# v for the pooled keys of the first two batches on all 128 partitions, both halves of v begun together, and an order planned with longer transfers

## The chip, the cores and the metric

The kernel runs on one core of a Trainium2 chip. The metric is the device time of one execution in microseconds. Three executions of the kernel before took 993.01, 996.15 and 1002.56 us; the median is 996.15 us. One further execution was profiled; it took 994.15 us, of which 991.8 us lie between its first and its last instruction (the span). All durations below come from that one execution.

## The reference, cut to what matters

There are 8 batches of 8 heads, 576 rows each of 64 numbers. Each head gets two attentions, and their outputs are added. The first averages q, k and v over groups of four rows (576 become 144), attends over all 144 pooled keys, and repeats each output row four times. The second attends only over keys at most three rows away. The sum, 4608 tokens of 512 numbers, goes through a two-layer network.

```python
q_d = q.reshape(B, H, Sd, factor, D).mean(axis=3)      # k_d and v_d alike; factor 4, Sd 144
out_d = sm_attn(q_d, k_d, v_d)
out_up = np.repeat(out_d, factor, axis=2)
scores = scale * np.matmul(q, k.transpose(0, 1, 3, 2))
scores = np.where(np.abs(pos[:, None] - pos[None, :]) < factor, scores, -1000000000.0)
out_local = np.matmul(softmax(scores), v)
x = (out_up + out_local).transpose(0, 2, 1, 3).reshape(4608, 512)
h = x @ w_in                                           # 512 x 2048
out = (h * np.clip(h + 3.0, 0.0, 6.0) / 6.0) @ w_out   # 2048 x 512
```

## The kernel before, in words

**Attention.** The work is cut into 32 units: batch b (0 to 7) and head pair hp (0 to 3). A unit keeps its two heads on the two halves of the partitions. `scores_d` (L401, L415 for later batches) multiplies pooled q with pooled k, `scores` (L569) multiplies windows of 64 rows for the local attention. Softmax follows: greatest value (L439) and sums (L448) on DVE (VectorE), exponentials on ACT (ScalarE; L435 pooled, L445 local), the tiny constant added on POOL (GpSimd, L451), the reciprocal on DVE (L454), the product with it on POOL or DVE (L457). Then the weights of the softmax are transposed, the pooled ones by L464 and the local ones by L592 on PE (TensorE) in batches 0 and 1 (`b < ALONE`). Later batches send them through DRAM (L476, L503 out; L484, L489, L510 back) and turn them on DVE (L498, L517). Last come the products with v (L543 pooled, L609 local), a scaling by a quarter on ACT (L548), and the addition of both outputs (`add`, L626) into x.

**v.** Each unit loads v twice. `ldv` loads the local windows: half h = 0 goes to partitions 0 to 63 as 64 x 5 x 128, half h = 1 to partitions 64 to 127 as 64 x 4 x 128 and 64 x 128. `ld4` loads the rows from which `sum4` (L369 on DVE, L371 and L372 on POOL) sums four and four. For batches 0 and 1 the 144 pooled keys stand as 72 and 72, even and odd keys, so these rows go to partitions 0 to 71 (`KB` is 72), and `trans_d` takes every second column.

**The network.** Tokens go in parts of 512, 256 and then 384 (`PART`). Each part has 16 first products (L864, one for each block of w_in, called wi0 to wi15) and 16 second products (L914, wo0 to wo15). All numbers are split into a high and a low fp32r part, so each product is three matmuls. `plan_split` makes the parts of x (high L119, low L791), L870, L874, L878 and L882 those of the hidden numbers.

**The weights.** A weight arrives as two 32-bit words (L161, 512 KB for a block of 128 x 512). ACT scales one word (L172 into a bank of PSUM, or L176 in place) and the other (L190), DVE puts the bits together (L181, L185), ACT rounds the high part (L195), POOL or DVE subtracts (L199). So each block costs ACT three instructions, and DVE two or three.

**What sets the order.** Every step is given to `Plan` with an engine, a cost in us, and what it waits for. `Plan.emit` runs a list schedule with these costs and writes each engine's instructions in the order that comes out. [...] `dma(packets, size)` is the cost of a transfer, `need(b)` the time at which a batch is wanted, `lag` an extra delay behind what a step waits for. While the plan sees PE idle at the start it fills the gap with matmuls that nobody reads (L947). `loads` lists the transfers of batch 0 for which the first `GATE` weight blocks wait; later blocks wait for the block `GATE` places ahead to be rounded. All transfers are issued by one engine, SP, in order. The tiles `early` are buffers of batch 0 that lie where weights go later; a0 to a2, o0 to o2, h0 and h1 are banks of PSUM.

## Time and profile before

| what | us |
|---|---|
| median of three runs | 996.15 |
| profiled execution | 994.15 |
| its span | 991.8 |
| PE busy in the span | 942.9 |
| DVE busy | 612.7 |
| ACT busy | 346.8 |
| POOL busy | 270.4 |

The page gives busy time by engine, 40 slices of the span with the busy share in tenths, the granted TensorE clock (PEclk) and what the transfers moved (GB/s), and the costliest groups. In an answer by time (a timeline), a row reads: start, duration, engine, line, operation, result and operands, and in square brackets how long the engine had idled before it and what ended that. In an answer on waits, a row reads: who waited for whom, us in total, how often, the longest. A table of stretches gives for each its length, then busy time of PE, PE's weight loads, DVE, ACT and POOL with the number of instructions, the granted clock (1.00 is full), the busy share of the transfer engines and GB/s.

### The profile page before, as it was taken

To read this page: it belongs to the slowest core of one execution; us is meant where nothing else is said; L and a number is where in the kernel's file an instruction comes from. 1 tells how busy PE (TensorE), PEld (TensorE's weight loads), DVE (VectorE), ACT (ScalarE), POOL (GpSimd) and SP (SyncE) were. 2 spreads that over 40 slices of the span, in tenths; PEclk is the share of its full clock that TensorE was granted. 3 is DMA by queue.
4 is the path that set the end of the run, shared out by engine and by line. 5 is a ranking of instruction groups with operands and counts; after the bars stand their busy time and mean duration, and the time that the engine had idled before them with its cause. 6 is when DMAs were issued, how large, how long until landed. Compare 5 with 4: busy or idle time off the path is not lost.

```text
span 991.8 us, 19738 instructions
## 1 busy us (share of the span) xinstructions
PE 942.9 (95%) x7493; PEld 811.4 (82%) x7493; DVE 612.7 (62%) x1147; ACT 346.8 (35%) x814; POOL 270.4 (27%) x370
## 2 busy tenths in 40 slices
PE   7689998997899999999999999999999999999997
PEld 4467776886788888888898888888898888998996
DVE  6688898677757576766736765766736753323322
ACT  4677664332322322322422322422322332322321
POOL 4644335123423223322402332432402320000000
PEclk9789999998999999999999999999999999999999
DMA  8977352456644545463524455453533430100101
GB/s 188 249 210 216 93 134 45 99 117 115 132 96 95 109 95 116 97 115 65 126 45 82 99 112 104 94 114 77 115 68 64 101 76 8 33 1 0 33 1 32
DMA packets 310974, 93.52 MB, mean 94 GB/s; under 512 B 251264, under 2 KB 297216, under 8 KB 310880
## 3 DMA queue, kind: packets, MB, share of 16 engines
q1 hardware_dynamic: 310880, 92.27, 42.6%
q8 instruction: 59, 0.97, 0.4%
q14 instruction: 35, 0.29, 0.1%
HBM read 69.60 MB, written 22.61 MB: 93 GB/s over the span
## 4 chain that ended last, share of the span: by engine, by line
PE 64%; SPq 11%; DMA 9%; DVE 9%; issue 3%; POOL 2%; ACT 2%; DVEq 0%; ACTq 0%; POOLq 0%
PE h L864 31%; PE o L914 28%; SPq L300 4%; DMA arena<-in_v_dram 3%; SPq L510 2%; SPq L484 1%; DMA arena<-pl 1%; DMA rawo<-in_w_out_dram 1%; SPq L489 1%; PE a L609 1%; DMA rawi<-in_w_in_dram 1%; PE a L569 1%; DVE arena L439 1%; DMA arena<-in_q_dram 1%; ACT arena L435 1%
## 5 line engine op out<-in xcount | busy, mean ns | idle before, releaser
L864 PE MATMUL h<-rounded,wi 128*128 128x384 f32 (+2 forms) x2240 | 438.4, 339 | 8.6 <-POOL rounded L791 3.7
L914 PE MATMUL o<-wo,rounded 128*128 128x512 f32 x1680 | 430.2, 396 | 4.9 <-ACT wo L195 1.2
L864 PEld LDWEIGHTS h<-rounded,wi 128*128 128x128 f32 x2240 | 391.6, 189 | 35.4 <-POOL rounded L791 4.0
L914 PEld LDWEIGHTS o<-wo,rounded 128*128 128x128 f32 x1680 | 308.1, 188 | 66.8 <-issue 4.2
L874 DVE SCALAR_TENSOR_TENSOR arena<-arena,h 128x384 f32<-128x384 f32 (+2 forms) x192 | 104.5, 546 | 154.5 <-ACT arena L870 153.8
L870 ACT ACTIVATE arena<-h 128x384 f32<-128x384 f32 (+2 forms) x192 | 94.0, 491 | 281.9 <-PE h L864 266.3
L878 ACT CAST rounded<-arena 128x384 fp32r<-128x384 f32 (+2 forms) x192 | 98.2, 513 | 173.7 <-DVE arena L874 116.6
L882 DVE TENSOR_TENSOR rounded<-arena,rounded 128x384 fp32r<-128x384 f32 (+2 forms) x154 | 90.0, 589 | 91.1 <-PE o L914 63.5
L882 POOL TENSOR_TENSOR rounded<-arena,rounded 128x384 fp32r<-128x384 f32 (+2 forms) x38 | 41.5, 1093 | 212.0 <-PE o L914 123.3
L435 ACT ACTIVATE arena<-a,arena 128x144 f32<-128x144 f32 x84 | 31.0, 377 | 101.2 <-DVE arena L430 82.0
L307 DVE STREAM_TRANSPOSE arena<-arena 128x576 f32<-128x576 f32 x56 | 42.7, 767 | 19.8 <-DMA arena<-in_q_dram 16.4
L442 POOL TENSOR_TENSOR arena<-arena 128x640 f32<-128x640 f32 x21 | 26.5, 1261 | 60.4 <-issue 36.3
L517 DVE STREAM_TRANSPOSE arena<-arena 128x640 f32<-128x640 f32 x24 | 20.2, 843 | 33.8 <-DMA arena<-pl 33.8
L609 PEld LDWEIGHTS a<-arena 64*64 64x64 f32 x1120 | 20.7, 134 | 20.9 <-ACT arena L435 8.6
L320 POOL TENSOR_TENSOR arena<-arena 128x144 f32<-128x144 f32 x23 | 12.0, 521 | 89.4 <-PE a L415 32.5
L451 POOL TENSOR_SCALAR arena<-arena 128x10 f32<-128x10 f32 (+1 forms) x60 | 16.7, 279 | 71.2 <-ACT arena L435 42.8
L609 PE MATMUL a<-arena 64*64 64x57 f32 (+1 forms) x1120 | 25.4, 223 | 11.1 <-ACT arena L435 7.6
L498 DVE STREAM_TRANSPOSE arena<-arena 128x384 f32<-128x384 f32 (+1 forms) x48 | 22.1, 466 | 17.1 <-DMA arena<-pd 16.5
L791 POOL TENSOR_TENSOR rounded<-arena,rounded 128x768 fp32r<-128x768 f32 x6 | 10.9, 1835 | 79.1 <-DVE rounded L121 79.1
L457 DVE TENSOR_TENSOR arena<-arena 128x432 f32<-128x432 f32 (+1 forms) x36 | 31.2, 868 | 0.9
L569 PE MATMUL a<-arena 64*64 64x64 f32 x1200 | 29.7, 226 | 0.5 <-ACT arena L119 0.5
L322 POOL TENSOR_TENSOR arena<-arena 128x144 f32<-128x144 f32 x46 | 28.7, 624 | 3.6
(182 smaller groups left out, 877.8 us busy)
## 6 DMA issues: line engine op xcount, KB each, us to landing
rawi<-in_w_in_dram SPq DMA_DIRECT2D x16, 512.0 KB
rawo<-in_w_out_dram SPq DMA_DIRECT2D x16, 512.0 KB
arena<-in_q_dram SPq DMA_DIRECT2D x112, 72.0 KB
arena<-in_k_dram SPq DMA_DIRECT2D x112, 72.0 KB
pl<-arena SPq DMA_DIRECT2D x24, 320.0 KB
arena<-pl SPq DMA_DIRECT2D x96, 80.0 KB
out_dram<-arena SPq DMA_DIRECT2D x96, 72.0 KB
arena<-in_v_dram SPq DMA_DIRECT2D x24, 256.0 KB
```

The lines of the kernel that those rows point to most:

```text
L300: nc.sync.dma_start(raw[32 * e:32 * e + 32], bass.AP(tensor=t.tensor, offset=t.offset + row0 * ROW + 32 * e, ap=[[ROW, 32], [32 * ROW, S / ...
L307: nc.vector.transpose(out=qk[kind], in_=st["raw", kind].rearrange("p j i -> p (j i)"))
L435: nc.scalar.activation(p[:, j], x[:, j], AF.Exp, bias=m[:, j:j + 1], scale=1.0 / 128.0, accum_out=s[:, j:j + 1])
L457: eng.tensor_tensor(x, x, s.unsqueeze(2).broadcast_to(list(x.shape)), op=ALU.mult)
L569: nc.tensor.matmul(st["ps", g][half:half + WIN, jj * D:jj * D + WIN], qk_of("q")[hs, k_first:k_first + WIN], qk_of("k")[hs, k_first:k_firs ...
L609: nc.tensor.matmul(st["px"][g][h * D:(h + 1) * D, at + lo:at + hi], st["v"][ks, jj, h * D:(h + 1) * D], st["pt"][ks, jj, half + lo:half + ...
L864: nc.tensor.matmul(st["ps"], win[f][:, wt, kk * P:(kk + 1) * P], xs[part][:, kk], start=(kk == 0 and i == 0), stop=(kk == NK - 1 and i == ...
L870: nc.scalar.activation(st["t"], st["ps"], AF.Relu, bias=3.0)
L874: nc.vector.scalar_tensor_tensor(out=t, in0=t, scalar=6.0, in1=st["ps"], op0=ALU.min, op1=ALU.mult)
L878: nc.scalar.copy(st["gh"], st["t"])
L882: eng.tensor_tensor(st["gl"], st["t"], st["gh"].bitcast(F32), op=ALU.subtract)
L914: nc.tensor.matmul(otile[n, m], gt[:, ms], wout[f][:, wt], start=(f == 0 and i == 0), stop=(f == NF - 1 and i == 2),)
```

## The change

The 144 pooled keys of batches 0 and 1 now stand as 128 and 16 in their own order, no longer as 72 and 72. So `ld4` loads the rows to be summed as one transfer to 128 partitions and one to 16, `sum4` makes sums of 128 and 16 partitions, `trans_d` takes columns 0 to 127 and 128 to 143, and `pv_d` multiplies over 128 and then 16. The number of instructions stays what it was on PE, DVE, ACT and POOL; batch 0 has one more transfer for each unit.

For batch 0 the second half of v no longer waits for the first, and both halves join `loads`. So the first ten weight blocks (`GATE` was 8) wait until all of batch 0 is loaded.

The plan's numbers change: `dma` costs 30% more, the pooled exponentials cost 1.74 in place of 1.0 (1.16 and 0.58 in place of 0.67 and 0.33 for later batches), ACT's first two steps on a weight come 2 us later (`LAGW`), and batch 1 is wanted 8 us sooner. The whole program is ordered anew by them.

```diff
-        a = op("ACT", 0.68, rebias, [ld], take=[place])
-        c = op("ACT", 0.68, low, [ld])
+        a = op("ACT", 0.68, rebias, [ld], take=[place], lag=LAGW)
+        c = op("ACT", 0.68, low, [ld], lag=LAGW)
...
         def ld4(g):
-            if b == 0:
-                raw = buf("raw4", ("v", un), [KB, 2, 4, ROW])
-                nc.sync.dma_start(raw, src(v_all, row0, [[8 * ROW, KB], [1, 8 * ROW]]))
-                st["raw", 0], st["raw", 1] = raw[:, 0], raw[:, 1]
-            elif alone:
-                st["raw", g] = raw = buf("raw" + k0, ("v", un, g), [KB, 4, ROW])
-                nc.sync.dma_start(raw, src(v_all, row0 + 4 * g, [[8 * ROW, KB], [1, 4 * ROW]]))
-            elif g == 0:
-                st["raw", g] = raw = buf("raw" + k0, ("v", un, g), [P, 4, ROW])
+            if b == 0 and "raw4" not in st:
+                st["raw4"] = buf("raw4", ("v", un), [P, 2, 4, ROW])
+            raw = st["raw4"][:, g] if b == 0 else buf("raw" + k0, ("v", un, g), [P, 4, ROW])
+            if g == 0:
                 nc.sync.dma_start(raw, src(v_all, row0, [[4 * ROW, P], [1, 4 * ROW]]))
             else:
-                st["raw", g] = raw = buf("raw" + k0, ("v", un, g), [NAR, 4, ROW])
-                for h in range(2):
+                n = 1 if alone else 2
+                raw = raw[:n * KR]
+                for h in range(n):
                     nc.sync.dma_start(
                         raw[h * KR:(h + 1) * KR], src(v_all, row0 + 4 * P, [[4 * ROW, KR], [1, 4 * ROW]]))
+            st["raw", g] = raw
...
-            lv.append(op("SP", 0.5, partial(ldv, h), lv[-1:], take=[("v" + kv, un)], size=dma(WIN * 5, 512), nd=1 + h))
+            lv.append(op("SP", 0.5, partial(ldv, h), [] if b == 0 else lv[-1:], take=[("v" + kv, un)], size=dma(WIN * 5, 512), nd=1 + h))
+        if b == 0:
+            loads.extend(lv)
...
-                nc.tensor.transpose(out=ps[:KB, j * P:(j + 1) * P], in_=st["pd"][:, j, g::2], identity=ident)
+                nc.tensor.transpose(
+                    out=ps[:nk[g], j * P:(j + 1) * P], in_=st["pd"][:, j, g * P:g * P + nk[g]], identity=ident)
...
-            sums_d = [op("ACT", 1.0, lambda: weigh(rows_d(), st["pd"], st["md"], st["sd"]), [a], free=[bk])]
+            sums_d = [op("ACT", 1.74, lambda: weigh(rows_d(), st["pd"], st["md"], st["sd"]), [a], free=[bk])]
...
-PRE, GATE = 4, 8
+PRE, GATE = 4, 10
...
+LAGW = 2.0
...
-    return start_of(need_chunk(b)) - (EARLY * TC if b and b % 2 == 0 else 0.0) - ((4.0, 16.0)[b] if b < ALONE else SLACK)
+    return start_of(need_chunk(b)) - (EARLY * TC if b and b % 2 == 0 else 0.0) - ((4.0, 24.0)[b] if b < ALONE else SLACK)
...
-    return packets * (5.0 + 0.0376 * size) / 16e3 if size > 256 else packets * (1.0 + 0.1 * size) / 16e3
+    return packets * (6.5 + 0.049 * size) / 16e3 if size > 256 else packets * (1.3 + 0.13 * size) / 16e3
```

What the new order does is shown at three places. Lines of the changed kernel are one or two off from those before (L443 is L445 before, L433 is L435, L455 is L457, L792 is L791, L865 is L864, L544 is L543, L593 is L592, L610 is L609).

The first place is ACT, where the first weight block comes in, about 20 us into the program. `rawi0` holds the words of block wi0. `early_318` and `early_353` before, `early_316` and `early_349` now, are the local scores of units 2 and 3 of batch 0. Before:

```order
L445 ACTIVATE early_201<-early_201 128x640
L119 COPY arena_65<-o1_277 128x3x128
L435 ACTIVATE early_231,arena_65<-a0_230,arena_65 128x144 x3
L172 ACTIVATE o0_348<-rawi0_271 128x512
L190 ACTIVATE rawi0_271<-rawi0_271 128x512
L176 ACTIVATE rawi1_281<-rawi1_281 128x512
L190 ACTIVATE rawi1_281<-rawi1_281 128x512
L172 ACTIVATE a2_402<-rawi2_293 128x512
L445 ACTIVATE early_318<-early_318 128x640
L435 ACTIVATE early_387,early_319<-a0_386,early_319 128x144 x3
L119 COPY arena_65<-o2_420 128x384
```

Now:

```order
L443 ACTIVATE early_194<-early_194 128x640
L119 COPY arena_65<-o0_276 128x3x128
L119 COPY arena_65<-o1_289 128x3x128
L433 ACTIVATE early_228,arena_65<-o2_227,arena_65 128x144 x3
L443 ACTIVATE early_316<-early_316 128x640
L433 ACTIVATE early_381,early_317<-o1_380,early_317 128x144 x3
L443 ACTIVATE early_349<-early_349 128x640
L119 COPY arena_65<-o2_427 128x384
L119 COPY arena_65<-a1_432 128x256
L172 ACTIVATE o1_458<-rawi0_345 128x512
L190 ACTIVATE rawi0_345<-rawi0_345 128x512
```

Five instructions on three weight blocks stood ahead of the exponentials of unit 2. Now the first of them stands behind those of unit 2, the local ones of unit 3, and both copies of unit 0's transposed weights (L119).

The second place is PE in the first part of tokens, around the first unit of batch 1: L464 transposes its pooled weights, L543 (L544) is their product with v, L592 (L593) transposes the local ones, L609 (L610) is their product with v. Before, the product with block wi4 stood behind the first transposes:

```order
L464 MATMUL a0_889<-ident_72,arena_65 72x128 x3
L464 MATMUL a2_896<-ident_72,arena_65 72x128 x3
L864 MATMUL h0_902<-rounded_66,wi4_738 128x512
L864 MATMUL h0_902<-lo_542,wi4_738 128x512
L864 MATMUL h0_902<-rounded_66,wi4_738 128x512 x2
```

Now:

```order
L865 MATMUL h0_834<-lo_568,wi2_727 128x512
L865 MATMUL h0_834<-rounded_66,wi2_727 128x512
L464 MATMUL a1_874<-ident_72,arena_65 128x128 x3
L464 MATMUL a0_879<-ident_72,arena_65 16x128 x3
L544 MATMUL a2_895<-arena_65 64x144 x4
L593 MATMUL a1_905<-ident_72,arena_65 128x128 x3
L593 MATMUL a0_909<-ident_72,arena_65 128x128 x2
L610 MATMUL a1_925<-arena_65 64x60 x2
```

The unit's four steps now follow each other directly behind block wi2; before, they stood behind wi3, with wi4 between the first and the second of them.

The third place is POOL ahead of the third part of tokens, whose x it splits (L791, L792). L320 and L322 pool q or k of a later unit, L457 (L455) is the softmax's product, and L368, L369, L373 and L374 sum v. Before:

```order
L320 TENSOR_TENSOR arena_65<-arena_65 128x144
L322 TENSOR_TENSOR arena_65<-arena_65 128x144 x2
L451 TENSOR_SCALAR arena_65<-arena_65 128x10
L320 TENSOR_TENSOR arena_65<-arena_65 128x144
L322 TENSOR_TENSOR arena_65<-arena_65 128x144 x2
L457 TENSOR_TENSOR arena_65<-arena_65 128x640
L791 TENSOR_TENSOR rounded_66<-arena_65,rounded_66 128x768
```

Now:

```order
L455 TENSOR_TENSOR arena_65<-arena_65 128x640
L368 TENSOR_TENSOR arena_65<-arena_65 32x256
L369 TENSOR_TENSOR arena_65<-arena_65 32x128
L373 TENSOR_SCALAR arena_65<-arena_65,head_77 32x64 x2
L374 MEMSET arena_65 32x128
L792 TENSOR_TENSOR rounded_66<-arena_65,rounded_66 128x768 x2
L440 TENSOR_TENSOR arena_65<-arena_65 128x640
L320 TENSOR_TENSOR arena_65<-arena_65 128x144
```

The split stood behind two poolings and a softmax product, and half of it was DVE's. Now both halves are POOL's, and they stand behind the sums of v and ahead of the next pooling.

More of the change, by code (lines that the diff above doesn't have):

```diff
@@ L380, in plan_unit @@
         for h in range(2):
[L381 removed]
+            lv.append(op("SP", 0.5, partial(ldv, h), [] if b == 0 else lv[-1:], take=[("v" + kv, un)], size=dma(WIN * 5, 512), nd=1 + h))
+        if b == 0:
+            loads.extend(lv)
         for g in range(2):
             rk = ("raw4", ("v", un)) if b == 0 else ("raw" + k0, ("v", un, g))
[L384 to L387 removed]
+            l = op("SP", 0.5, partial(ld4, g), take=[rk], size=dma((P, KR if alone else NAR)[g], 2048), nd=1 if alone else 1 + g)
+            if b == 0:
+                loads.append(l)
             sums.append(early_user(op(
```

25 lines of the change are left out of this document (11 added, 14 removed).

## The prediction

> **What bounds the kernel now.** I read the page's shares first, then the granted clock and the transfers along the span, then a table of stretches, then the waits of the stretches in which PE is idle.
>
> ```profile
> span 991.8 us, 19738 instructions
> PE 942.9 (95%) x7493; PEld 811.4 (82%) x7493; DVE 612.7 (62%) x1147; ACT 346.8 (35%) x814; POOL 270.4 (27%) x370
> ...
> 20.00:60.00 40.00, 27.43 (x387) 17.99 (x384) 28.54 (x64) 25.52 (x64) 25.91 (x40) 0.86 0.99 227
> 60.00:130.00 70.00, 68.79 (x504) 53.33 (x505) 60.98 (x108) 48.32 (x101) 26.78 (x32) 0.96 0.50 153
> 130.00:180.00 50.00, 44.18 (x321) 32.97 (x320) 44.33 (x68) 24.69 (x53) 23.22 (x22) 0.97 0.47 105
> 180.00:300.00 120.00, 109.68 (x1044) 95.81 (x1044) 80.87 (x163) 36.81 (x100) 38.63 (x58) 0.97 0.54 109
> 300.00:992.00 692.00, 678.01 (x5093) 600.99 (x5091) 385.38 (x720) 203.64 (x485) 150.20 (x204) 1.00 0.36 74
> ```
>
> PE is busy 942.9 of 991.8 us, so 48.9 us are the most that any reordering could save, short of a faster clock. Of that, 12.6 us lie between 20 and 60, 7.0 between 60 and 180, 10.3 between 180 and 300, and 14.0 in all the rest from 300 on, the last stores included. From 60 to 130 PE is 98% busy and DVE 87%; there a step that comes late has little room to be caught up, but also little to lose. The change touches the first two batches by its layout and everything by its order, so the places to look at are the stretches ahead of 300.
>
> **What ends last between 20 and 60.** The waits of that stretch, longest first, then the rows of ACT, PE and DVE at the place:
>
> ```profile
> ACT o L172 <- DMA rawi<-in_w_in_dram: 6.7, 1, 6.7
> ...
> PE a L592 <- ACT early L435: 6.2, 1, 6.2
> DVE early L448 <- ACT early L445: 4.1, 1, 4.1
> ...
> DVE early L369 <- DMA early<-in_v_dram: 2.4, 1, 2.4
> ```
>
> ```profile
> 29.54 0.63 ACT L172 ACTIVATE o<-rawi 128x512 f32<-128x512 f32 x1 [6.74 <-DMA rawi<-in_w_in_dram]
> ...
> 31.56 0.67 ACT L176 ACTIVATE rawi<-rawi 128x512 f32<-128x512 f32 x1 [0.82 <-DMA rawi<-in_w_in_dram]
> ...
> 33.60 0.62 ACT L172 ACTIVATE a<-rawi 128x512 f32<-128x512 f32 x1 [0.82 <-DMA rawi<-in_w_in_dram]
> 34.16 0.72 ACT L445 ACTIVATE early<-early 128x640 f32<-128x640 f32 x1
> ```
>
> ```profile
> 29.22 0.55 PE L592 MATMUL o<-ident,arena 128*128 128x128 f32 x3 [0.84 <-POOL arena L457]
> 36.01 0.69 PE L592 MATMUL a<-ident,arena 128*128 128x128 f32 x2 [6.25 <-ACT early L435]
> ```
>
> These belong together. ACT takes its instructions in order. It sat 6.74 + 0.82 + 0.82 = 8.38 us before the first three weight blocks, and the exponentials of unit 2 (L445, L435) stood behind them. PE could not finish the transposes of unit 0, because the bank that it needed was freed by that L435, so PE lost 6.25 us and DVE 4.1 us. This is a stall of order, not of work.
>
> **Part one: ACT's order at the start.** In the new order the weights' first instruction stands behind the exponentials of unit 2, the local ones of unit 3, and unit 0's copies. The 6.25 us go. Late next is the softmax product on POOL that released PE at 29.22, so PE can go on from there at once. The gain lies between 6.25 us (PE's wait) and 8.38 us (ACT's three waits, since the copies behind PE's transposes also found ACT occupied with weights). I take 7, nearer to PE's row, because PE is what the end follows. A second stall of the same kind sits at 55.88:
>
> ```profile
> 55.88 0.70 ACT L176 ACTIVATE rawi<-rawi 128x512 f32<-128x512 f32 x1 [2.19 <-DMA rawi<-in_w_in_dram]
> ...
> 60.14 5.79 PE h L864 x12
> ...
> 101.32 2.73 PE h L864 x12
> ```
>
> There ACT waited for wi7's words, with the high part of the last quarter of x (L119) two instructions behind. The new order puts ACT's weight steps 2 us later, and issues batch 0's v sooner, so I count 1.5 of the 2.19 us; bounds 0 and 2.19. The first full product of the network took 5.79 us where later ones take 2.73, since the clock was low from 59 to 66 (the row on that stretch stands below); I count no gain from it, as any new wait of PE would bring it back.
>
> Against this stands what PE's new order does around batch 1's first unit.
>
> ```profile
> 66.26 0.81 PE L569 MATMUL a<-arena 64*64 64x64 f32 x40
> ...
> 76.77 0.90 PE L592 MATMUL a<-ident,arena 128*128 128x128 f32 x5
> ```
>
> From its local scores to the transposes of their softmax 10.5 us passed before, with wi2, wi3 and wi4 between. Now only half of wi0, and wi1 and wi2 stand between: a quarter of 2.73 for each of wi0's pieces, some 1.4 at most, and 2 x 2.73, so 6.1 to 6.9 us. If the softmax's chain is as long as it was, PE waits 3.6 to 4.4 us there. Since block wi3 is due later in DVE's order than before, part of this wait would have come anyway. Bounds 0 and 4.4; I take 2.
>
> So part one is 7 + 1.5 - 2 = 6.5 us. Does it stay? The work between 60 and 180 is the same, and it starts sooner on PE and on DVE alike, since DVE's stalls (4.1 and 2.4) go with PE's. It is lost where weights come later than now; that is a rival below.
>
> **Part two: the x of the third part of tokens.** The waits of PE from 165 to 300, and the stretch after the second part with POOL's rows:
>
> ```profile
> PE h L864 <- POOL rounded L791: 3.7, 1, 3.7
> PE a L609 <- ACT arena L435: 2.9, 1, 2.9
> PE a L609 <- issue: 2.4, 2, 1.6
> ```
>
> ```profile
> 232.01 0.45 POOL L320 TENSOR_TENSOR arena<-arena 128x144 f32<-128x144 f32 x1 [0.83 <-DVE arena L307]
> 232.55 1.20 POOL L322 TENSOR_TENSOR arena<-arena 128x144 f32<-128x144 f32 x2
> 233.70 1.26 POOL L457 TENSOR_TENSOR arena<-arena 128x640 f32<-128x640 f32 x1
> 234.92 1.80 POOL L791 TENSOR_TENSOR rounded<-arena,rounded 128x768 fp32r<-128x768 f32 x1
> ```
>
> ```profile
> 59.00:66.00 7.00, 6.70 (x15) 3.99 (x16) 6.62 (x12) 4.98 (x13) 1.64 (x2) 0.52 0.98 372
> ...
> 234.00:240.00 6.00, 3.23 (x10) 3.03 (x11) 5.74 (x10) 0.00 (x0) 2.72 (x2) 0.50 0.40 71
> ```
>
> POOL split x only after a pooling that had waited for DVE's transpose. PE waited 3.71 us, and then ran its 3.23 us at half the clock, which cost another 1.6. In the new order the split stands ahead of that pooling, and PE has blocks wo13 and wo14 ahead of the third part in place of wo13 alone. On the other side POOL now makes both halves, 2 x 1.80 us, and sums of v stand before them. Bounds 0 and 3.7 + 1.6 = 5.3; I take 3.
>
> **Part three: the later units' distance.** Between a unit's scores and its product with v its softmax goes through DRAM. I counted PE's instructions between the two, in both orders, for the second, third and fourth unit of batch 2, with the durations of these rows:
>
> ```profile
> 194.28 1.39 PE o L914 x6
> 195.66 1.43 PE h L864 x12
> ...
> 276.00 2.08 PE h L864 x12
> 278.09 2.08 PE o L914 x9
> ```
>
> With 1.5 us for another unit's product with v and 1.1 for its scores, the sums are 22, 19 and 25 us before, and 24, 31 and 27 us now. The waits of these units are 1.61, 0.78 (together the 2.4 of the row on L609 and issue) and 2.9 us. The added 2, 12 and 2 us would cover 1.6 + 0.8 + 2 = 4.4 us. But SP, which issues the transfers, also serves other units in a new order, so not all of it comes; bounds 0 and 4.4, I take 2.5. The plan's dearer exponentials and transfers do nothing on the chip but this. Past 300 PE has 14 us of idle time, mostly the end; I count nothing there, with 2 us either way.
>
> **The layout itself.** PE, DVE, ACT and POOL issue as many instructions as before, with the same number of elements in a partition; the sums of 72 partitions become sums of 128 and of 16. I cost that at nothing: what a row of this profile takes goes by its elements in a partition, and if it didn't, these few sums lie on POOL beside ACT and PE. Batch 0 has four more transfers. What the layout may change is how fast v comes in. The stretches, with the transfers' busy share and GB/s as the last two figures:
>
> ```profile
> 4.00:11.00 7.00, 5.30 (x21) 3.52 (x19) 3.78 (x9) 2.38 (x3) 1.57 (x3) 1.00 0.98 289
> 11.00:26.00 15.00, 11.83 (x218) 8.41 (x218) 10.63 (x21) 6.99 (x19) 9.25 (x17) 1.00 0.96 153
> ...
> 32.00:35.00 3.00, 0.00 (x0) 0.00 (x0) 0.09 (x1) 2.18 (x5) 1.13 (x2) 0.50 1.01 403
> ```
>
> From 4 to 11 the q and k of batch 0 go to all partitions, from 32 to 35 weights do; from 11 to 26 the loads of v go to 64 or 72 partitions, and move half as much at the same busy share. At 153 GB/s the 15 us are 2.3 MB. At the 289 of q and k these would take 8 us, 7 fewer. The rows of v are also shorter (512 bytes), so the trace doesn't separate the two causes. In the new order all 20 transfers of v stand ahead of the first weight block, which waits for them. Before, 0.2 MB of v followed the first block, which now precedes it: 1.3 us at 153, and I put another 1 us on waiting for the last of it. So at 289 the first block would land some 5 us before the 29.54 of now, at 153 some 2 us after. ACT now asks for it later than it did, at about 31 us (unit 0's copies, 29.22 + 0.55 + 0.69 and their own 0.9), so either way little waits for it. Hence this is no term of the sum, only a condition on part one.
>
> The Trainium skill (DMA: Bandwidth & Descriptors, Rules for kernel authors) speaks against beginning both halves together: "Two transfers to disjoint partition halves: Don't bother — they serialize", for both spread over the same 16 transfer engines. The half rate of the 153 GB/s row at a full busy share says that something else than engines limits a half; no run here shows two halves at once. By the rule the sum would be that of the third case below.
>
> **The sum.** 994.15 - 6.5 - 3 - 2.5 = 982.15 us. The profiled execution lies 2 us below the median of 996.15 and 1.1 above the lowest run; I add 1 and say 983.
>
> **The rivals.**
> 1. The forecast: 983 us. Bounds of its terms: at best 8.4 + 2.2 + 5.3 + 4.4 = 20.3 us, 975; at worst 6.25 - 4.4 = 1.9, 993. Chance 0.50.
> 2. Part one is given back before 180: DVE, 87% busy from 60 to 130, can't deliver wi3 and the blocks behind it sooner, and PE waits there instead. For it: the lumped unit of batch 1, and wi3 behind that unit's additions in DVE's order. Against it: DVE, too, gains its 4.1 and 2.4 us. Half of parts two and three remain: 995.15 - 3 = 992. Chance 0.27.
> 3. The halves don't go faster together. Everything that hangs on v (the sum of unit 3 on DVE, the first weights) comes 2 us later than now, and ACT's weight steps eat about 3 us of part one: 986. For it: the short rows; against it: the 153 beside 289. Chance 0.12.
> 4. Slower than before: ACT's order stalls more than it did. Between unit 0's copies and the last quarter of x stand ACT's steps on six weight blocks. The later ones are issued behind the eight transfers of batch 1's q and k:
>
> ```profile
> 29.64 5.80 SPq L300 DMA_DIRECT2D arena<-in_q_dram  x4
> 35.54 4.58 SPq L300 DMA_DIRECT2D arena<-in_k_dram  x4
> ```
>
> If each of the six waits 2.2 us, as wi7 did, that is 13.2 us, less the 7 gained, and PE at half clock for such a stretch adds 3.2 (59 to 66 above): 9.4 us, so 1005 us. It decides where block wi3 lands after ACT gets to it, by my count of ACT's rows some 10 us behind unit 0's copies, at about 41. By the old times it would be issued at 35.54 + 4.58 = 40.1, too late; with v in 5 us sooner at 35, in time. Chance 0.11.
>
> **How the numbers follow.** The likeliest case gives 983. A measurement of this kernel can tell about 1% from no change, so faster is below 986.2 and slower above 1006. Faster: 0.43 of case 1, half of case 3, a hundredth of case 2: 0.50. Slower: 0.07 of case 4. The same: the other 0.43. The range goes from 972 (case 1 at its best, with the clock kept high between 59 and 66, 3 us more) to 998, which takes in case 2 and leaves out most of case 4.
>
> **What would show it.** Part one: ACT shows no wait of several us for w_in's words ahead of L443, PE no 6 us wait at L593, and the first full product of wi1 starts at 51 to 55 us, not at 60. If it starts there and part one of tokens still ends at the old 178, case 2 holds. Part two: no wait of 3 us for POOL's L792 between 200 and 260. Part three: fewer than 3 us of waits at L610 there. The layout: the stretch that loads v moves well over 153 GB/s; if not, case 3. Case 4 shows as waits of ACT for words of weights between 30 and 50, and a first full product after 60.

## The result

The changed kernel took 967.52 us (median of 966.26, 966.68, 968.36 and 969.68), the kernel before 997.5 beside it. The ratio is 0.970, with a 95% interval of 0.965 to 0.975. That is 30 us faster; the forecast was 983 us, in a range from 972 to 998. The profiled execution of the changed kernel took 966.26 us.

### The profile page after: what moved, and what is told of

Read it like the earlier page. It is cut to its first block, busy times and chain, and to the rows that moved or that the text cites. A ratio compares the mean times of both kernels' runs of the same rounds, so it can differ in the third digit from the quotient of the medians.

```text
span 964.5 us, 19717 instructions
## 1 busy us (share of the span) xinstructions
PE 936.4 (97%) x7503; PEld 810.5 (84%) x7503; DVE 591.5 (61%) x1131; ACT 343.2 (36%) x805; POOL 287.9 (30%) x385
## 4 chain that ended last, share of the span: by engine, by line
PE 79%; SPq 6%; DVE 4%; DMA 4%; POOL 3%; issue 2%; ACT 1%; DVEq 0%; POOLq 0%; ACTq 0%
PE h L865 35%; PE o L915 35%; PE a L610 2%; SPq L300 2%; PE a L570 1%; SPq L485 1%; PE a L915 1%; DMA arena<-in_k_dram 1%; PE a L413 1%; SPq L490 1%; PE a L533 1%; DMA rawo<-in_w_out_dram 1%; DMA arena<-pl 1%; DMA arena<-pd 1%; SPq L511 1%
## 5 line engine op out<-in xcount | busy, mean ns | idle before, releaser
L865 PE MATMUL h<-rounded,wi 128*128 128x384 f32 (+2 forms) x2240 | 432.8, 337 | 0.9 <-DVE arena L875 0.8
L865 PEld LDWEIGHTS h<-rounded,wi 128*128 128x128 f32 x2240 | 390.7, 189 | 23.7 <-issue 1.8
L871 ACT ACTIVATE arena<-h 128x384 f32<-128x384 f32 (+2 forms) x192 | 94.5, 492 | 313.8 <-PE h L865 281.9
L883 POOL TENSOR_TENSOR rounded<-arena,rounded 128x384 fp32r<-128x384 f32 (+2 forms) x55 | 60.3, 1098 | 250.7 <-PE o L915 118.7
L883 DVE TENSOR_TENSOR rounded<-arena,rounded 128x384 fp32r<-128x384 f32 (+2 forms) x137 | 77.9, 571 | 87.4 <-PE o L915 61.0
L433 ACT ACTIVATE arena<-a,arena 128x144 f32<-128x144 f32 x84 | 31.2, 378 | 94.8 <-DVE arena L428 80.7
L455 POOL TENSOR_TENSOR arena<-arena 128x640 f32<-128x640 f32 (+1 forms) x38 | 41.8, 1111 | 17.1 <-DVE arena L452 15.5
L366 DVE TENSOR_REDUCE arena<-arena 128x128 f32<-128x512 f32 (+2 forms) x34 | 36.5, 1073 | 4.8 <-PE a L533 4.3
L792 POOL TENSOR_TENSOR rounded<-arena,rounded 128x768 fp32r<-128x768 f32 (+2 forms) x9 | 12.4, 1396 | 86.7 <-DVE rounded L121 86.7
L440 POOL TENSOR_TENSOR arena<-arena 128x640 f32<-128x640 f32 x23 | 29.0, 1262 | 27.9 <-DVE arena L437 16.2
L610 PEld LDWEIGHTS a<-arena 64*64 64x64 f32 x1140 | 21.0, 137 | 12.1 <-issue 3.6
L320 POOL TENSOR_TENSOR arena<-arena 128x144 f32<-128x144 f32 x24 | 11.1, 463 | 64.6 <-PE a L413 22.8
L322 POOL TENSOR_TENSOR arena<-arena 128x144 f32<-128x144 f32 x48 | 28.3, 589 | 3.8
```

Of the source, the lines that this page charges most:

```text
L366: eng.tensor_reduce(out=vd, in_=raw.rearrange("p r e -> p e r"), op=ALU.add, axis=AX.X)
L433: nc.scalar.activation(p[:, j], x[:, j], AF.Exp, bias=m[:, j:j + 1], scale=1.0 / 128.0, accum_out=s[:, j:j + 1])
L455: eng.tensor_tensor(x, x, s.unsqueeze(2).broadcast_to(list(x.shape)), op=ALU.mult)
L610: nc.tensor.matmul(st["px"][g][h * D:(h + 1) * D, at + lo:at + hi], st["v"][ks, jj, h * D:(h + 1) * D], st["pt"][ks, jj, half + lo:half + ...
L865: nc.tensor.matmul(st["ps"], win[f][:, wt, kk * P:(kk + 1) * P], xs[part][:, kk], start=(kk == 0 and i == 0), stop=(kk == NK - 1 and i == ...
L871: nc.scalar.activation(st["t"], st["ps"], AF.Relu, bias=3.0)
```

## The profile after

The page of the changed kernel, and the table of stretches with the same bounds as before (columns as there; in the changed kernel weights are among the transfers of its first row from 21.1 us on):

```profile
span 964.5 us, 19717 instructions
...
PE 936.4 (97%) x7503; PEld 810.5 (84%) x7503; DVE 591.5 (61%) x1131; ACT 343.2 (36%) x805; POOL 287.9 (30%) x385
...
PEclk9979998999999999999999999999999999999999
```

```profile
11.00:26.00 15.00, 12.91 (x212) 8.18 (x202) 14.53 (x32) 8.24 (x25) 12.66 (x24) 1.00 0.80 210
20.00:60.00 40.00, 31.37 (x420) 21.11 (x415) 36.23 (x77) 29.50 (x72) 30.50 (x41) 0.97 0.92 244
60.00:130.00 70.00, 67.65 (x467) 53.49 (x466) 58.60 (x102) 48.33 (x98) 26.32 (x28) 0.95 0.66 175
130.00:180.00 50.00, 47.55 (x396) 38.49 (x394) 36.48 (x66) 20.82 (x46) 18.51 (x20) 0.93 0.39 83
180.00:300.00 120.00, 119.19 (x1134) 105.09 (x1133) 84.65 (x174) 39.54 (x108) 52.03 (x76) 1.00 0.58 114
```

PE's idle time, the span less its busy time, went from 48.9 to 28.1 us. Its busy time also fell, from 942.9 to 936.4, though it runs ten instructions more. The two falls, 20.8 and 6.5 us, make up the 27.3 us by which the span became shorter.

The ten instructions are matmuls that nobody reads, with which the plan fills gaps at the start (before, then now):

```profile
L947 PE MATMUL h<-identb 128*128 128x512 bf16 x25 | 8.1, 440 | 3.0 <-DVE identb L143 3.0
L948 PE MATMUL h<-identb 128*128 128x512 bf16 x35 | 9.7, 408 | 2.8 <-DVE identb L143 2.8
```

So PE's busy time holds 8.1 and 9.7 us that are not work. Of the idle time that went at the start, 1.6 us were only filled, and the work itself took 8.1 us less.

Stretches with fixed bounds compare different work once one kernel runs ahead. The next two tables are therefore cut where the work of PE changes: at the end of the first product of the first, second, third and fourth part of tokens (the start of L870, L871 now, on it). First the kernel before, then the changed one:

```profile
0.00:60.00 60.00, 42.21 (x537) 28.26 (x537) 41.15 (x92) 33.37 (x78) 31.57 (x54) 0.91 0.96 217
60.00:177.60 117.60, 110.98 (x812) 84.73 (x812) 103.39 (x172) 71.94 (x151) 50.00 (x54) 0.96 0.48 132
177.60:240.60 63.00, 55.97 (x550) 48.23 (x551) 44.98 (x95) 21.02 (x62) 18.61 (x29) 0.95 0.51 106
240.60:326.00 85.40, 80.08 (x759) 70.01 (x758) 57.60 (x109) 25.73 (x68) 29.46 (x41) 1.00 0.54 108
326.00:991.80 665.80, 653.63 (x4838) 580.12 (x4837) 365.58 (x684) 194.77 (x461) 140.75 (x193) 1.00 0.35 74
```

```profile
0.00:48.60 48.60, 40.13 (x591) 26.19 (x591) 42.55 (x94) 30.42 (x78) 33.32 (x54) 1.00 0.89 231
48.60:167.70 119.10, 110.03 (x772) 86.18 (x772) 98.71 (x171) 72.20 (x148) 51.00 (x55) 0.93 0.57 150
167.70:220.40 52.70, 52.70 (x509) 46.91 (x511) 33.80 (x75) 20.10 (x58) 19.77 (x29) 1.00 0.49 101
220.40:299.30 78.90, 78.09 (x751) 68.53 (x751) 55.32 (x109) 23.92 (x61) 32.71 (x48) 1.00 0.64 124
299.30:964.50 665.20, 655.42 (x4893) 582.70 (x4891) 361.16 (x685) 196.54 (x465) 151.06 (x201) 1.00 0.35 74
```

Length less PE's busy time gives the idle time of each stage:

| stage | idle before | idle after | saved |
|---|---|---|---|
| start, to the first product | 17.8 | 8.5 | 9.3 |
| first part of tokens | 6.6 | 9.1 | -2.5 |
| second part | 7.0 | 0.0 | 7.0 |
| third part | 5.3 | 0.8 | 4.5 |
| the rest | 12.2 | 9.8 | 2.4 |

So 9.3 of the 20.8 us were saved at the start, of which the first part of tokens lost 2.5 again. More than half was saved in the second and third part, which I call the middle below: 12.3 us of idle time before, 0.8 after. The waits of PE from 160 to 325, the longest of before and all of after, show the middle directly:

```profile
PE a L609 <- ACT arena L435: 4.5, 2, 2.9
PE h L864 <- POOL rounded L791: 3.7, 1, 3.7
PE a L609 <- issue: 2.4, 2, 1.6
```

```profile
PE o L915 <- POOL wo L199: 0.8, 1, 0.8
PE h L865 <- DVE arena L875: 0.8, 1, 0.8
```

In the start, ACT now comes to the first weight without a wait (27.50 us, behind unit 0's copies), and at the transposes of unit 0's local weights PE waits 1.88 us, where it waited 0.84 and then 6.25:

```profile
26.05 0.55 PE L593 MATMUL o<-ident,arena 128*128 128x128 f32 x3 [1.88 <-POOL arena L455]
```

```profile
27.24 0.38 ACT L119 COPY arena<-a 128x256 f32<-128x256 f32 x1
27.50 0.66 ACT L172 ACTIVATE o<-rawi 128x512 f32<-128x512 f32 x1
```

The lead of 11.4 us at the first product grows to 13.7 by the third, and is then all spent on batch 1's first unit, whose steps stand together behind wi2; wi3's product begins at 68.17, at a low clock (0.66 on average from 57 to 72):

```profile
55.45 0.88 PE L464 MATMUL a<-ident,arena 128*128 128x128 f32 x6 [1.48 <-POOL arena L455]
59.06 1.42 PE L544 MATMUL a<-arena 128*64 128x144 f32 x8 [2.74 <-DVE arena L121]
62.12 1.49 PE L610 MATMUL a<-arena 64*64 64x60 f32 x38 [0.38 <-ACT arena L119]
66.96 0.30 PE L562 MATMUL a<-maskb,identb 128*128 128x320 bf16 x1 [1.97 <-DVE arena L627]
```

These are 6.6 us of waits. The kernel before runs its own such unit later, so of the 13.7 us some 10 remain when the second part of tokens begins (177.6 before, 167.7 after).

## The experiments

All ratios are to the kernel before, run beside them on the same chip. "Idle in the middle" is PE's idle time in the second and third part, from tables cut like those above. Theory N is the prediction's own: the order by the plan's numbers brings the gain, the layout by itself nothing. Theory V gives the start's share to the layout.

### Numbers alone, layout alone

The first kernel has only the plan's numbers of the change (`dma`, `LAGW`, the exponentials' costs, `GATE`, `need`), the second only the layout and the loosened halves. The diff leads from the changed kernel to the second; its reverse, in the kernel before, gives the first.

```diff
-LAGW = 2.0, GATE 10, need(1) 24.0, exponentials 1.74 / 1.16 / 0.58, dma(6.5, 0.049)
+LAGW = 0.0, GATE 8,  need(1) 16.0, exponentials 1.0 / 0.67 / 0.33,  dma(5.0, 0.0376)
```

> The old layout (72 and 72, second half of v behind the first) with all the new numbers of the plan. Theory N, the prediction's own (the gain comes from the order that the numbers give, the layout is worth nothing by itself): 965 to 973 us, first product of wi1 before 53, as in the changed kernel. Theory V (the start's 11 us come from v being in sooner, which only the layout and the loosened halves give; the numbers bring what follows from 180 on, about 14 us): 978 to 986 us, the stretch that loads v stays near 153 GB/s, first product of wi1 at 57 us or later. Theory S (the numbers and the layout were chosen together, and an order made for one doesn't fit the other): over 990 us.

> The new layout and the loosened halves with all the old numbers of the plan. Theory N: 990 to 998 us, ACT's wait of several us for the first weight is back. Theory V: 982 to 988 us, v in by 22 us, the first weight's words there some 4 us sooner, so that PE's wait of 6.25 us shrinks to 2 or 3 although the weights still stand ahead of the exponentials; from 180 on the time runs as before the change. Theory S: within 3 us of the kernel before, with new waits at other places.

The numbers alone took 978.68 us (ratio 0.981, 0.978 to 0.984), the layout alone 983.6 (0.985, 0.982 to 0.989). Both lie where theory V had them. With the layout alone the first product was done at 50.8 us, 9.2 sooner than before; with the numbers alone at 56.2 (V had said 57 or later), and the stretch from 11 to 26 moved 164 GB/s, against 208 with the layout. In these two runs the sooner start goes with the layout; further kernels of both kinds below make that weaker. But V had given the middle to the numbers, and neither kernel had more than half of that: idle in the middle was 7.7 us with the numbers and 6.8 with the layout (12.3 before, 0.8 after).

### The halves of v

```diff
-lv.append(op("SP", 0.5, partial(ldv, h), [] if b == 0 else lv[-1:], ...))
+lv.append(op("SP", 0.5, partial(ldv, h), lv[-1:], ...))
-        if b == 0:                      # these two lines only in the first of the two kernels
-            loads.extend(lv)
```

> The changed kernel, but the second half of v again waits for the first in the plan, and no weight waits for the halves of v. 128 and 16 and all numbers stay. By the rule that two halves serialize anyway, and by theory N: 965 to 970 us, the same rate while v is loaded. Theory V: 971 to 978 us, v's last piece some 5 us later, under 170 GB/s between 11 and 20 us.

> The changed kernel, but in batch 0 the plan starts each second half of v only when the first is in; the weights still wait for all of v. So the four first halves are issued together and the four second halves behind them. If two halves of the partitions serialize, or if only the 128 partitions of the other loads made v faster: v in as early as in the changed kernel (first weight's transfer issued within 1 us of 21.1), 965 to 971 us. If halves must alternate to load fast: first weight issued 3 us or more later, under 170 GB/s from 11 to 20 us, 970 to 977 us. Both pieces of the third part's split stand on POOL here, so by theory P PE's idle time in the second and third part stays under 2 us; by theory D it may be anything up to 8.

The first took 973.63 us (0.975, 0.973 to 0.978), which was V's figure, but for another reason than V's: v did not come slower (218 GB/s from 11 to 26, weights from 19.6 us on among it, since they no longer stand behind all of v), the start was as quick (first product at 50.5), and the loss is in the middle, with 7.7 us of idle time: this order gives one half of the third part's split of x to DVE, on which more below. The second kernel took 965.57 us (0.966, 0.963 to 0.970), as fast as the changed kernel, though it issues its last load of v at 22.9 us and its first weight at 23.5, not at 20.6 and 21.1. So beginning both halves together is worth nothing that can be measured in the kernel's time. The Trainium skill (DMA: Bandwidth & Descriptors, Rules for kernel authors) says of two transfers to disjoint halves that they serialize and aren't worth it; the time agrees. What is left is why v became faster; these are the packets of the transfers from 11 to 20 us, of the kernel before, the changed one, the one with chained halves, and one with the old layout and the new numbers (the first kernel of the last group below):

```profile
DMA packets 1278, 1.38 MB, mean 153 GB/s; under 512 B 89, under 2 KB 1068, under 8 KB 1277
q1 hardware_dynamic: 1277, 1.36, 101.5%
```

```profile
DMA packets 2380, 1.61 MB, mean 179 GB/s; under 512 B 220, under 2 KB 2063, under 8 KB 2379
q1 hardware_dynamic: 2379, 1.59, 78.2%
```

```profile
DMA packets 1976, 1.74 MB, mean 193 GB/s; under 512 B 181, under 2 KB 1460, under 8 KB 1975
q1 hardware_dynamic: 1975, 1.72, 98.5%
```

```profile
DMA packets 1235, 1.56 MB, mean 174 GB/s; under 512 B 94, under 2 KB 967, under 8 KB 1234
q1 hardware_dynamic: 1234, 1.55, 88.5%
```

The second row of each is the queue's packets, its MB, and their time as a share of sixteen engines. Before, the engines were busy all the time with 1.36 MB, so 1.36 MB / (16 x 9 us x 1.015) = 9.3 bytes a ns for each; in the changed kernel 14.1, and with chained halves 12.1. The loads to 128 partitions are common to both of the latter. But the fourth has none of these, and 12.2. Over all kernels of this document, one profile each, the nine with the old layout moved 8.6 to 12.2 bytes a ns for each engine, the eleven with the new one 12.1 to 15.3. So the new layout goes with faster loads, and the order in which the loads are issued counts as well; how the two work was not tried.

### ACT's delay, the prediction's part one

```diff
-LAGW = 2.0                                   # in the changed kernel
+LAGW = 0.0
-a = op("ACT", 0.68, rebias, [ld], take=[place])            # in the kernel before, c alike
+a = op("ACT", 0.68, rebias, [ld], take=[place], lag=2.0)
```

> The changed kernel with the 2 us of delay for ACT's first steps on a weight set to 0. Theory N (part one of the prediction is the place of these steps in ACT's order): 973 to 977 us, ACT waits 3 us or more for the first words with the exponentials of unit 2 behind it, PE 4 us or more at L593. Theory V: 966 to 970 us, since the words are there when ACT comes to them.

> The kernel before with nothing but the 2 us of delay for ACT's first steps on a weight. The prediction's part one by itself, without the later v: 6.5 us gained, so a ratio of 0.9935 to the kernel before, first product of wi1 at 53 to 55. Theory V (without the new layout the words of v and of the weights come as late as before, and ACT's new order only moves the wait): a ratio of 0.996 to 1.003, first product of wi1 at 57 to 61.

Without the delay the changed kernel took 968.92 us (0.969, 0.966 to 0.973): in time nothing is lost, as V had it. The first weight again stands ahead of the exponentials (L443) on ACT, but since v is in early its words are almost there, and the wait is 1.44 us, not 6.74:

```profile
26.92 0.63 ACT L172 ACTIVATE o<-rawi 128x512 f32<-128x512 f32 x1 [1.44 <-DMA rawi<-in_w_in_dram]
27.48 0.72 ACT L443 ACTIVATE early<-early 128x640 f32<-128x640 f32 x1
```

The start is not the same, though. ACT comes to the first product only at 57.7 us (48.6 with the delay), and PE is idle for 12.2 us until then (8.5 with it). The first part of tokens then has 5.0 us of idle time, where the changed kernel has 9.1, and the second part begins at 164.5, 3.1 us sooner than there.

The delay alone in the kernel before gave 984.52 us (0.985, 0.980 to 0.990), more than either theory had. Its waits of PE up to 62 us show that the place of the prediction's part one was right and its price was not:

```profile
PE h L864 <- ACT wi L195: 4.4, 1, 4.4
...
PE a L265 <- DMA rows<-in_q_dram: 2.5, 1, 2.5
PE o L401 <- POOL early L322: 2.2, 1, 2.2
```

The 6.25 us at L592 are gone, but PE waits 4.4 us for the weight that now comes later, and the first product was done at 58.8 us, 1.2 sooner than before. The lead appeared later: 4.4 us at the second part of tokens, 9.2 at the fourth, 9.9 at the last product with w_in. Nothing in the edit aims there.

### The engine that splits the third part's x

In the changed kernel POOL makes both halves of that split (L792), before it and DVE made one each. One line gives the split to an engine; the order up to there stays.

```diff
+                if n == 2:                       # kernel before; in the changed one: n == 2 and k, "DVE"
+                    eng_lo = {"POOL": eng_lo["POOL"]}
```

> The kernel before, with one more rule for the plan: both halves of the third part's split of x (L791) are POOL's; before, POOL made one and DVE the other. All engines keep their order up to that split, the plan orders what follows anew. Theory P (the engine of this split decides the stretch from 180 to 300, where the change took 11.5 us of PE's idle time away): idle time of PE in the second and third part of tokens falls from 12.3 to under 4 us, the time by 7 to 10 us against the kernel before. Theory D (that stretch needs more than this: the softmax of the units and the second weights come too late also, so the order as a whole): the wait of 3.7 us for L791 is replaced by another of its kind, idle time stays at 8 us or more, the time within 4 us of the kernel before.

> The changed kernel, with the second half of the third part's split of x (L792) given to DVE alone; first half on POOL as before. All engines keep their order up to that split. Theory P: PE waits 2 to 3 us for that half and again some 3 us for the hidden numbers that DVE makes behind it (as in the kernel with the new numbers and the old layout), the time is 972 to 978 us. Theory D: 967 to 971 us, since all else of the order is kept.

The changed kernel with one half on DVE took 972.21 us (0.974, 0.970 to 0.978). That is 4.7 us more, or 3.6 by the ratios, whose intervals overlap. Its middle has 4.5 us of idle time in place of 0.8, nearly all in one wait:

```profile
PE h L868 <- DVE rounded L792: 4.0, 1, 4.0
```

So theory P's mechanism holds there, at the price of this one wait; the 3 us behind it, which P had also named, did not come. In the kernel before, giving POOL both halves brought only 3 us (996.92; 0.997, 0.995 to 1.000). The 3.7 us for L791 went, a longer wait took their place, and the middle kept 11.6 us of idle time:

```profile
PE o L917 <- DVE rounded L885: 6.5, 2, 5.4
```

That is theory D. One step set right in a poor order uncovers the next one.

These two kernels also show how much two executions of one order differ, since each keeps the order of its model up to that split. Their first products came at 62.3 and 50.8 us, where the profiled executions of their models have 60.0 and 48.6. So some 2 us of a difference at the start, read from one profile each, can be execution alone.

### Controls: the same kernels, drawn again

The delay alone had gained without a reason that its trace shows. So I moved a number of the plan by an amount that means nothing, and let it order the program again; the fourth run is a real part of the change alone.

```diff
-packets * (5.0 + 0.0376 * size)         # kernel before: 3% more
+packets * (5.150 + 0.03873 * size)
-((4.0, 16.0)[b]                         # kernel before: batch 1 wanted 1 us sooner
+((4.0, 17.0)[b]
-packets * (5.0 + 0.0376 * size)         # kernel before: the change's 30%
+packets * (6.5 + 0.049 * size)
-op("ACT", 1.74, ...), op("ACT", 1.16 - 0.58 * i, ...)      # changed kernel: 3% more
+op("ACT", 1.79, ...), op("ACT", 1.19 - 0.60 * i, ...)
```

> The kernel before with the plan's transfers 3% longer, too little to mean anything by itself; it orders the program anew from batch 1's v on. A control. Theory R (the kernel before had drawn a poor order, and any other draw of the planner is better by some 10 to 15 us): a ratio of 0.98 to 0.99. Theory K (the numbers do what they say, a delay here, longer transfers there): a ratio of 0.996 to 1.004, PE's idle time in the second and third part of tokens stays at 10 us or more (12.3 before).

> The kernel before with batch 1 wanted 1 us sooner (the change: 8 us), a second control; the order is the same up to PE's 453rd instruction, in the first part of tokens, and new from there. Theory R: a ratio of 0.985 to 0.993, since only what follows is drawn anew. Theory K: 0.996 to 1.004.

> The kernel before with the plan's transfers 30% longer, as in the change, and nothing else. Both pieces of the third part's split of x stand on POOL in this order. Theory K: what the units wait for their softmax at L609 from 180 to 300 (4.5 and 2.4 us before) falls under 2.5 us in all, PE's idle time in the second and third part to under 5 us, a ratio of 0.985 to 0.992, while the start is as before (first product of wi1 at 58 us or later). Theory R: as in the controls, whatever they give.

> The changed kernel with the plan's pooled exponentials 3% dearer, a control from the other side. Its order puts one piece of the third part's split of x on DVE. Theory R (the changed kernel is a lucky draw): 972 to 980 us. Theory K: 965 to 971 us, but for the piece on DVE, which by the run with that piece given to DVE costs 4.7 us, so up to 973.

The two redraws of the kernel before took 988.56 us (0.991, 0.988 to 0.994) and 990.62 (0.993, 0.991 to 0.995); that of the changed kernel 974.23 (0.977, 0.973 to 0.982). All three lie outside what theory K allows, the third only just, since its order puts half of the third part's split on DVE. But that, too, came from the draw. Theory R's figures hold for the second and third, and are missed by 0.001 in the first. A draw of the order, with nothing behind it, moved this kernel by 7 to 9 us. This also limits the single runs above: the changed kernel with chained halves, without the delay, or with one half on DVE differs from the changed kernel by 1.4 to 6.1 us, less than one such draw. The 30% gave 980.01 us (0.982, 0.978 to 0.986), but not by K's mechanism: PE still waited at L609, as its waits from 160 to 325 show, and idle time in the middle was 7.3 us although both halves of the split are POOL's. Its start, too, was another, with the first product at 55.6 us where K had 58 or later.

```profile
PE a L609 <- issue: 4.2, 2, 2.7
PE a L609 <- DMA arena<-in_v_dram: 1.5, 1, 1.5
```

### Layout and numbers, several draws each

To tell the parts from the draws, each mixture of old and new got two small changes of the same kind: `dma` 3% more, or batch 1 wanted 1 us sooner.

```diff
-packets * (6.5 + 0.049 * size)          # new numbers
+packets * (6.700 + 0.05038 * size)
-((4.0, 24.0)[b]
+((4.0, 25.0)[b]
-packets * (5.0 + 0.0376 * size), ((4.0, 16.0)[b]           # old numbers
+packets * (5.150 + 0.03873 * size), ((4.0, 17.0)[b]
```

> The old layout with all the new numbers, and the plan's transfers 3% longer still: a second draw of the kernel with the numbers alone (978.7 us in its first). Theory A (layout and numbers each bring their own part, some 8 and 14 us, and every draw of the order adds 5 us up or down): 974 to 984 us. Theory R (draws alone): as wide as all draws so far, 965 to 998, with no place of its own. Theory S (layout and numbers fit each other): over 984. Both pieces of the third part's split stand on POOL here; by theory P PE's idle time in the second and third part is under 3 us.

> The old layout with all the new numbers, batch 1 wanted 1 us sooner still: a third draw of the same kind. Theory A: 974 to 984 us. Theory R: anywhere from 965 to 998. The third part's split stands half on DVE, as in the first draw: by theory P idle time of 6 us or more in the second and third part.

> The new layout and the loosened halves with the old numbers, but the plan's transfers 3% longer: a second draw of the kernel with the layout alone (983.6 us in its first). Theory A: 979 to 989 us, v in by 22 us and the first product of wi1 at 49 to 54 us, as the layout gives. Theory R: anywhere from 965 to 998.

> The new layout and the loosened halves with the old numbers, but batch 1 wanted 1 us sooner: a third draw of the same kind, alike up to PE's 684th instruction. Theory A: 979 to 989 us. Theory R: anywhere from 965 to 998.

> The changed kernel with the plan's transfers 3% longer still: a third draw of it (967.5 us in its first, 974.2 in its second). Theory A: 965 to 977 us. Theory R (the first draw was lucky): 972 us or more. Both pieces of the third part's split stand on POOL here; by theory P PE's idle time in the second and third part is under 3 us.

> The changed kernel with batch 1 wanted 1 us sooner still: a fourth draw of it. Theory A: 965 to 977 us. Theory R: 972 us or more. The third part's split stands half on DVE, so by theory P 972 or more as well, with PE's idle time in the second and third part at 4 us or more.

They took 968.19, 985.63, 990.95, 983.98, 968.29 and 972.59 us. The first three lie outside the ranges of theory A, the first below and the other two above: A took 5 us for the bound of a draw, and it is about one standard deviation. The first, for which theory S had over 984, speaks against S. It also had 3.7 us of idle time in the middle, where theory P said under 3, and the third had its first product at 55.9 us, where A said 49 to 54. As ratios, with the earlier runs:

| | old numbers | new numbers |
|---|---|---|
| old layout | 1 (before), 0.991, 0.993: mean 0.995 | 0.981, 0.970, 0.987: mean 0.979 |
| new layout | 0.985, 0.992, 0.985: mean 0.987 | 0.970 (after), 0.977, 0.971, 0.977: mean 0.974 |

The spread within a cell is 0.0053 (one standard deviation). The numbers bring 0.0157 with the old layout and 0.0136 with the new, some 15 us; the layout brings 0.0073 and 0.0052, some 6 us. Each of the two parts, averaged over both columns or rows, has a standard error of 0.003, so the numbers' part is sure, and the layout's is two errors from nothing. The parts add up: nothing of theory S, and not draws alone either. The kernel before lies 5 us above the mean of its cell, the changed one 4 us below that of its own. So of the 30 us about 21 belong to the change, with a standard error of 4, and 9 to the two draws.

The first product shows where the layout's part lies. It was done at 60.0, 56.2 and 60.7 us with old layout and old numbers, at 56.2, 58.1 and 58.5 with the new numbers alone, at 50.8, 55.9 and 55.7 with the new layout alone, and at 48.6, 51.3, 51.7 and 49.5 with both. On average the layout brings 4.8 and 7.3 us there, the numbers 1.4 and 3.8. The clock may have a hand in it. The first and the third kernel with the layout alone have the same order on PE, DVE, ACT and POOL up to that product, and on SP up to 24 us, and yet are 4.9 us apart. The same stretch of both, the third below the first:

```profile
30.00:40.00 10.00, 9.04 (x150) 5.69 (x152) 9.48 (x25) 9.25 (x29) 7.92 (x12) 1.00 1.02 207
30.00:40.00 10.00, 8.71 (x80) 5.66 (x77) 7.08 (x18) 7.41 (x24) 6.50 (x11) 0.54 0.73 163
```

PE was busy nearly as long, but at a granted clock of 0.54 it came through 80 matmuls and not 150. Whether the low clock or the transfers fell behind first is not shown.

Among the orders with the new numbers, the place of the third part's split still tells them apart. With both halves on POOL the ratios are 0.966 to 0.971 (five kernels, one with the old layout, one without the delay) and idle time in the middle 0.8 to 3.7 us; with one half on DVE 0.974 to 0.987 (six kernels) and 4.5 to 8.4 us. Five of these six show the same three waits, here in the last run:

```profile
PE h L865 <- DVE arena L875: 3.2, 1, 3.2
PE h L865 <- DVE rounded L792: 2.5, 1, 2.5
PE a L610 <- ACT arena L433: 1.7, 1, 1.7
```

No run showed a kernel that is surely faster than the changed one: the best, with chained halves, is at 0.966 beside 0.970, with intervals that overlap.

## Why the prediction was wrong

The direction was right, the size was not: 12 us by the profile were forecast, 27.9 came. Step by step:

- **Part one, forecast 6.5 us.** Start and first part together saved 9.3 - 2.5 = 6.8 us of idle time. The figure came out, but by luck: its errors offset. The start saved 9.3 us, near its upper bounds (8.38 + 2.19), though 1.6 of these were only filled and some 2 can be execution. The lumped unit of batch 1 cost 6.6 us of waits where I had put 2, at most 4.4. The cause was named wrongly as well: ACT's order was to bring it, and its delay alone made the first product only 1.2 us sooner, while without the delay the time stayed the same. I had written that the layout is "only a condition on part one". On average it brings 4.8 and 7.3 us at the first product (old numbers, new numbers). ACT's wait for the first words, 6.74 us before, is 1.7 to 3.5 us in the three kernels with the new numbers alone, 3.4 to 4.7 in the three with the new layout alone, and at most 0.5 in the four with both.
- **The clock, forecast nothing but a share of part two (1.6 us of its bound).** This is the first term that failed. PE's busy time fell by 6.5 us, and by 8.1 without the matmuls that nobody reads. Length times what is missing from full clock, in the tables by stage, is 13.3 us before and 8.3 after, so at most some 5 us of the fall go with the clock: the low stretches at the start and in the second part are gone, and one at the lumped unit has grown. This count is rough, since idle time is in it and the tables give the clock to 0.01; the rest of the fall stays open. That "any new wait of PE would bring it back" came true for that unit, but I had weighed only the stretches from 59 to 66 and from 234 to 240. My ceiling of 48.9 us for any reordering was too low as well: it took the 8.1 us of matmuls that nobody reads for work.
- **Part two, forecast 3 us.** The mechanism holds: undone by itself it brings a wait of 4.0 us and costs 3.6 to 4.7, within the bounds of 0 to 5.3, though no more than a draw. Done by itself in the kernel before it brought the 3 us, but uncovered another wait.
- **Part three, forecast 2.5 us, and with it the sum over the middle.** This is the second term that failed. Parts two and three together were 5.5 us; 11.5 us of idle time went, more than even their upper bounds of idle time, 3.7 + 4.4. I had taken about half of the waits that I had listed, and the smaller ones (1.2, 1.1 and several of half a microsecond) not at all. The count of PE's work between scores and product was not tested alone. The 30% that I held responsible did not remove these waits by itself. Which of the plan's numbers clears the middle stays open; shown is that with all of them it is nearly clear where POOL has both halves of the split, and that neither the layout nor that split alone does it.
- **Past 300, forecast 0, 2 either way.** Idle time fell by 2.4 us, but PE's busy time there rose by 1.8. The lead was 26.7 us at the fourth part, 25.5 at the last product with w_in and 27.3 at the end of the span.
- **The layout, forecast nothing.** Some 6 us over three and four draws, though with an error of 3; they lie at the start, by the first products.
- **The rivals.** The second was right in its mechanism (the start's lead is spent at the lumped unit), but not in its place: it was spent ahead of wi3 and not behind it, and what came in the middle was twice the forecast instead of half. The third fell: the halves indeed bring nothing together, but v came faster all the same. The fourth fell: ACT's longest wait for weights before 60 us was one of 2.70.

Against the forecast, 6.5 us of busy time, 11.5 - 5.5 = 6.0 in the middle, 2.4 at the end and 0.3 at the start are 15.2 us, and 0.6 us lie outside the span; the profiled executions differ from the sum by 982.15 - 966.26 = 15.9.

What failed in the range is another thing. Its low end, 972, came from the terms' bounds for one order. But the plan draws the order of the whole program anew, and such a draw moves the time by 5 us (one standard deviation) without any cause in the change. The range had no term for that. By the means of the draws the change is worth 21 us, where 12 were forecast in the profile, so the sum was too small by some 8 or 9 us, two standard errors. With the 21 alone the time would have been about 977 us, inside the range; the 9 us of the two draws carried it below. The signs that I had named came in all the same, the first product even before the 51 us that I gave for it. They told which waits would go, and not how many others would go with them.

## What to carry to other kernels

Where a planner or scheduler orders the whole program, measure first how much a meaningless nudge of its numbers moves the time, and judge every change of the plan against several nudged copies of both kernels, not against one. A sum over the waits that one sees in one order is then good for the direction and the places, but its range needs that spread as a term of its own. And take a stall of order back to the transfer behind it: once the words came sooner, the delay on ACT no longer decided the time (968.92 us without it, 967.52 with it).

## What was not expected of the hardware

In the kernel before, loads whose destination is only 64 or 72 partitions kept the transfer engines busy all the time from 11 to 20 us, at 9.3 bytes a ns each. In the changed kernel, with loads to 128 partitions among them, an engine moved 14.1 while busy. Over all kernels the two kinds nearly part, at 8.6 to 12.2 and 12.1 to 15.3, so a full busy share by itself says little of how fast the engines move. The Trainium skill (DMA: Bandwidth & Descriptors, Why a DMA increments its semaphore by 16 and not by 1) says that a transfer is spread over the largest number of engines up to 16 that divides its outer dimension on both sides; by that rule 72 partitions would get 12, which is an estimate. No view here tells the engines apart, and a busy share of 101.5% doesn't look like idle engines. So it stays open whether the slow packets come from that, from the smaller number of partitions, or from the longer rows (4096 bytes in place of 2048); none of these was tried alone.
